# An attention, MLP and routed-expert kernel: new transfer times in the planner of the routed part, later take-up of weights, low parts on one engine, a regrouped end

## The chip, the cores and the metric

One core of a Trainium2 chip runs the whole program. The metric is the device time of one execution, in microseconds; a profiled execution is also given, with the span from its first to its last instruction. The engines are named as the profile names them: PE (TensorE matmul), PEld (its weight loads), DVE (VectorE), ACT (ScalarE), POOL (GpSimd) and SP (SyncE, which issues most transfers).

## What is computed

Windowed attention with memory tokens, then a two-layer MLP with leaky ReLU, then eight experts of which each token takes exactly one. The experts are filled by a greedy pass over all (token, expert) scores in falling order, each expert up to `cap = 384` tokens, so which expert a token gets can't be told from its own scores alone.

```python
def _moe2_ref(x, w_gate, w1, w2):              # x: 3072 x 512, E = 8, F = 1024
    logits = x @ w_gate
    order = np.argsort(-logits.flatten())
    for idx in order:
        tok, e = int(idx) // E, int(idx) % E
        if assigned[tok] >= 0 or counts[e] >= cap:
            continue
        assigned[tok] = e
        counts[e] += 1
    for e in range(E):
        mask = assigned == e
        out[mask] = np.maximum(x[mask] @ w1[e], 0.0) @ w2[e]
```

## The kernel before, in words

All matmuls of the MLP and the experts are made of three passes on rounded operands: a high part and a low part of each operand, high by high, high by low and low by high. A high part is an ACT copy, a low part is the difference, usually on DVE.

Nothing of the order of work is written out by hand. Every step is handed to a planner (`Plan`) with the engine it runs on, an assumed duration in microseconds, its dependencies and a priority (`key`, smaller first). `Plan.run` plays the assumed durations through and emits the instructions of each engine in the order in which the play starts them. On the chip every engine then works strictly through its own list and waits by semaphores. An assumed duration therefore changes no work, only the order of the lists. Transfers are played as ops of a single engine "D", one after the other, first ready first, and land 1.1 us plus the D time after their issue. `late=` adds to the time at which an op is held to be ready; `after=` lets an op be placed only once the named ops have been placed.

The change touches the routed part, `phase2`. For each expert in the order in which they fill up (p = 0 to 7):

- `search(p)` finds which expert fills next and at which score, by six rounds of threshold search. A round is a chain of small steps between DVE and PE: `differ` (tile d), `compare` (cm), `count` on PE (L311, pc), `less` (lc), `threshold` (fl), `base` on PE (L332, pb). It has the highest priority. Search p+1 starts when search p is done; the last expert needs none.
- `number(p)` reads the expert's number into a register of SP, `tail(p)` turns the tokens' places into indices (sl, sp, A, rh, then `tokens` on PE at L458), gathers 384 rows (`xg`, three transfers from POOL, L473), transposes them on PE (L478) and writes high and low parts (ACT `xth` L481, DVE `xtl` L485). These parts together are `XT[p]`, and every gemm1 of the expert waits for them.
- `load(p, f)` fetches slice f of eight (w1 and w2 slice side by side, 512 KB) into a ring of four `west` buffers, or for p = 0 as two halves into a ring of three. ACT makes the high part (L590) and DVE or POOL the low part (L591), two halves each. The weights of an expert alternate between two places, so they carry the names `wh`, `wl` (odd p) and `winh`, `winl` (even p).
- `gemm1(p, f)` is 12 matmuls (L608); ACT and DVE turn the result into `egh` (L614) and `egl` (L615). `gemm2(p, f)`, two slices later, is 9 matmuls (L631), three for each of the three tiles i of 128 tokens, which gather over all f in three accumulators.
- With the last slice each tile is copied out by ACT (`x`, L641) and stored row by row by POOL (L646), a 1x1 memset (L645) ahead of each store.

Priorities: loads have `200 + 8p + f - 6`, gemm1 `200 + 8p + f`, gemm2 two more; searches, tails and numbers are far below zero. While the MLP ends and the routed part's first rows come in, 40 matmuls that compute nothing (L659) keep PE going.

Of the kernel before, what the change touches and what calls it, by code (L numbers as in the profile page):

```python
# [15 lines left out]
AF = mybir.ActivationFunctionType  # L16
# [198 lines left out]
def phase2(tc, P, C, ident, L, x2d, we, out, ps_h, ps_o, ps_y, pools, lready, xready, open_pools, open_experts, room, roomy, before):  # L215
# [7 lines left out]
    NTILE, E = L.shape[1], L.shape[2]  # L223
    DM = out.shape[1]
    KD = DM // 128
    NF = we.shape[2]
    TT = NTILE // E
    TB = TT * 128
    FMAX = 3.4e38
    LASTV = 5  # L230
    LATE, SLACK = 0.3, 0.7
    SW = 0.12
    V, G, S = nc.vector, nc.gpsimd, nc.scalar
# [186 lines left out]
    def ranks(p):  # L420
        r = R[p]
        r["ps"] = pools["ps_t"].tile([128, 1], FT, name="pt")
        nc.tensor.matmul(r["ps"], C[0]["tri"], r["fx"][:, NTILE:], start=True, stop=True)

    def slots(p):

        r = R[p]
        b = rt([128, NTILE], FT, "sb")
        a = rt([128, NTILE], I16, "sl")
        V.tensor_scalar(b, r["fx"][:, :NTILE], r["ps"], 32.0, op0=OP.add, op1=OP.add)  # L430
        V.tensor_tensor(a, b, r["F"], op=OP.mult)
        s = r["sl"] = rt([128, 2, NTILE], I16, "sp")
        V.tensor_scalar(s[:, 0], a, 31, None, op0=OP.bitwise_and)
        V.tensor_scalar(s[:, 1], a, 5, None, op0=OP.logical_shift_right)

    def places(p):
        c, r = C[0], R[p]
        W = NTILE // PACK
        r["A"] = rt([128, PACK, 32, W], F16, "A")
        V.tensor_tensor(r["A"], c["i32"][:, :, :W][:, None].to_broadcast([128, PACK, 32, W]),  # L440
                        r["sl"][:, 0].rearrange("p (a b) -> p a b", a=PACK)[:, :, None, :]
                        .to_broadcast([128, PACK, 32, W]), op=OP.is_equal)

    def parts(p):
        c, r = C[0], R[p]
        oc = rt([128, 12, NTILE], F16, "oc")
        V.tensor_tensor(oc, c["i32"][:, 1:13], r["sl"][:, None, 1].to_broadcast([128, 12, NTILE]), op=OP.is_equal)
        r["rh"] = rt([128, 12, NTILE], F16, "rh")
        V.tensor_tensor(r["rh"], oc, c["token"][:, None, :].to_broadcast([128, 12, NTILE]), op=OP.mult)

    def tokens(p):

        r = R[p]
        W = NTILE // PACK
        r["px"] = pools["ps_t"].tile([128, PACK, TT, 4], FT, name="pt")
        A, rh = r["A"], r["rh"].rearrange("p n (a b) -> p a n b", a=PACK)
        for j in range(W):
            nc.tensor.matmul(r["px"], A[:, :, :, j].rearrange("p a m -> p (a m)"), rh[:, :, :, j],  # L458
                             start=(j == 0), stop=(j == W - 1))

    def indices(p):
        r = R[p]
        r["idx"] = rt([128, TT], I32, "idx", 4)
        s = rt([32, 2, TT, 4], FT, "ix")
        blk = lambda a: r["px"][32 * a:32 * a + 32, a]
        V.tensor_scalar(s[:, 0], blk(0), float(HALF), None, op0=OP.add)
        V.tensor_tensor(s[:, 1], blk(1), s[:, 0], op=OP.add)
        V.tensor_tensor(s[:, 0], blk(2), s[:, 1], op=OP.add)
        for n in range(4):
            V.tensor_tensor(r["idx"][32 * n:32 * n + 32], blk(PACK - 1)[:, :, n], s[:, 0, :, n], op=OP.add)  # L470
# [5 lines left out]
    def transpose(b, x):  # L476
        for d in range(KD):
            nc.tensor.transpose(b.t[:, d * 128:(d + 1) * 128], x.t[:, d * 128:(d + 1) * 128], ident)  # L478
# [23 lines left out]
    X, XT = {}, {}  # L502

    def small(us, fn, deps, use=(), late=0.0):

        return P.op(("T", us + SW), fn, deps, use, early=SW, late=late)
# [27 lines left out]
    def tail(p):  # L534
        P.key = -1000 + 10 * p + (1 if p else -1)
        late = SLACK if p else 0.0
        o = small(0.04, lambda: ranks(p), [filled[p], tchain], late=late)
        o = P.op(("V", 0.67), lambda: slots(p), [o])
        ts = [P.op(("V", 0.47), lambda: places(p), [o]), P.op(("V", 0.6), lambda: parts(p), [o])]
        o = small(0.53, lambda: tokens(p), ts, late=late)  # L540
        o = P.op(("V", 1.25), lambda: indices(p), [o])
        gathered[p] = o
        xg, gs = [], []
        for i in range(TT):
            x = r_xg[i].take()
            g = P.op(("G", 1.25), lambda i=i, x=x: gather(p, i, x), [o, xready, open_experts], [x])
            d = P.op(("D", 0.73), None, (), [x])
            P.dep(d, [g], lat=4.6 if p else 2.9)
            xg.append(x)
            gs.append(d)  # L550
        X[p] = [r.take() for r in r_xt]
        XT[p] = []
        for i in range(TT):
            b = ps_h.take() if p == 0 and i else Buf(lambda: pools["ps_t"].tile([128, DM], FT, name="pt"), None, None)
            o = small(0.44, lambda i=i, b=b: transpose(b, xg[i]), [gs[i], [] if p == 0 else o], [xg[i], b], late=late)
            a = P.op(("S", 0.5), lambda i=i, b=b: xhi(i, b, X[p]), [o], [X[p][0], b])
            o = P.op(("V", 0.6), lambda i=i, b=b: xlo(i, b, X[p]), [a], [*X[p], b])
            XT[p] += [a, o]
        tchain[:] = [o]


    W, REG = {}, {}
# [7 lines left out]
        REG[p] = P.op(("Q", 2.0), fn, [filled[p]])  # L570

    def load(p, f):
        P.key = 200 + NF * p + f - 6
        w = [r.take() for r in r_w[f]]
        n = 2 if p == 0 else 1
        d = []
        for b in [(ps_y if p == 0 else r_west).take() for _ in range(n)]:
            c = slice(1024 // n * len(d), 1024 // n * (len(d) + 1))

            def fn(b=b, c=c):  # L580
                src = we[bass.ds(R[p]["reg"], 1)].rearrange("a p f d -> (a p) f d")
                nc.sync.dma_start(b.t, src[:, f, c])

            d.append((b, P.dma(1.46 / n, fn, [REG[p]], [b], [open_experts if p else roomy[f]])))
        o = []
        for h in range(2):
            sl = slice(512 * h, 512 * h + 512)
            b, l = d[h % n]
            raw = lambda b=b, h=h: b.t if n == 2 else b.t[:, 512 * h:512 * h + 512]
            a = P.op(("S", 0.53), lambda sl=sl, raw=raw: S.activation(w[0].t[:, sl], raw(), AF.Copy), [l], [b, w[0]])  # L590
            o.append([a, P.op({"G": 1.22, "V": 0.6} if p == 0 else {"V": 0.6, "G": 1.22} if p > LASTV else {"V": 0.6}, lambda e=V, sl=sl, raw=raw: e.tensor_tensor(  # L591
                w[1].t[:, sl], raw(), w[0].t[:, sl].bitcast(FT), op=OP.subtract), [a], [b, *w])])
        W[p, f] = w, o

# [26 lines left out]
    def gemm2(p, f):  # L621
        s = NF * p + f
        P.key = 200 + s + 2
        w, o = W[p, f]
        gh, gl, done = GL.pop(s)
        if f == 0:
            ACC[p] = [r.take() for r in ps_o]

        def mm(i, n):
            l, a = ((gh, 0), (gh, 1), (gl, 0))[n]  # L630
            nc.tensor.matmul(ACC[p][i].t, l.t[:, 128 * i:128 * i + 128], w[a].t[:, 512:1024],  # L631
                             start=(f == 0 and n == 0), stop=(f == NF - 1 and n == 2))

        for i in range(TT):
            for n in range(3):
                q = PREV[i] = P.op(("T", 0.231), lambda i=i, n=n: mm(i, n), [done[:1 + n // 2], o[1], PREV.get(i)],
                                   [ACC[p][i], gh, gl, *w])
            if f < NF - 1:
                continue
            y = ps_y.take()  # L640
            o2 = P.op(("S", 0.53), lambda i=i, y=y: S.activation(y.t, ACC[p][i].t, AF.Copy), [q], [ACC[p][i], y])  # L641

            def fn(i=i, y=y):
                if stores:
                    G.memset(rt([1, 1], FT, "spacer"), 0.0)  # L645
                st = G.indirect_dma_start(  # L646
                    out=out, out_offset=bass.IndirectOffsetOnAxis(ap=R[p]["idx"][:, i:i + 1], axis=0),
                    in_=y.t, in_offset=None)
                for other in stores:
                    tc.declare_no_dep(st.ins, other.ins, reason="a token has one expert: rows of other tokens")  # L650
                stores.append(st)

            o2 = P.op(("G", 1.04), fn, [o2], [y])
            P.dep(P.op(("D", 0.73), None, (), [y]), [o2], lat=1.2)


    b, o = ps_h.take(), before
    for _ in range(40):
        prev, o = o, P.op(("T", 0.22), lambda b=b: nc.tensor.matmul(b.t[:, :128], ident, ident, start=True, stop=True),  # L659
                          (), [b], key=1e6)  # L660
# [603 lines left out]
```

## Time and profile before

| | us |
|---|---|
| three runs | 1025.14, 1026.04 (median), 1030.17 |
| the profiled execution's own time | 1028.83 |
| its span | 1027.0 |
| PE busy, of the span | 990.3 (96%) |
| DVE busy | 779.9 (76%) |
| ACT busy | 440.9 (43%) |
| POOL busy | 145.6 (14%) |
| chain that ended last: share of PE, DVE, transfers | 74%, 11%, 6% |

The routed part is the last 337 us of the span: its first gemm1 stands at 689.8, its last matmul at 1018.8. Busy shares here say little, since matmuls overlap in the records. What says more is the timeline of PE with the idle time ahead of each instruction and its releaser, and then, for each such gap, the timeline of the engine that released it, followed backwards.

### The profile page before, as it was taken

How to read it: one execution, taken by the hardware profiler on the slowest of the kernel's cores; microseconds unless marked ns; L12 is line 12 of the kernel's file. 1: busy time of each engine (PE TensorE's matmuls, PEld its weight loads, DVE VectorE, ACT ScalarE, POOL GpSimd, SP SyncE). 2: the span in 40 equal slices, each digit the busy share in tenths (PEclk: the TensorE clock that was granted, in tenths of full speed). 3: DMA queues.
4: the chain of work that ended last, by engine and by line, in shares of the span. 5: the costliest groups of instructions: out<-in, count | busy, mean ns of one | idle time of the engine just before them, and what ended most of it. 6: DMA issues, size and time to landing. Idle time of an engine off the chain costs nothing.

```text
span 1027.0 us, 17361 instructions
## 1 busy us (share of the span) xinstructions
PE 990.3 (96%) x6052; PEld 861.3 (84%) x6052; DVE 779.9 (76%) x2631; ACT 440.9 (43%) x1183; POOL 145.6 (14%) x155
## 2 busy tenths in 40 slices
PE   8799999999999999999999999989999999899996
PEld 7687888888888888888889988778778787788895
DVE  7999798788788698798788664688786887867610
ACT  6677634434434434543544333043342523326411
POOL 1677520000000000000000000011111211112311
PEclk9799999999999999999999999999999999989998
DMA  7666510110111120120120000155152432508400
GB/s 240 217 217 215 188 51 30 60 57 29 60 57 29 50 67 29 43 74 29 31 68 1 1 1 32 52 175 174 52 195 76 170 135 102 195 32 281 139 31 31
DMA packets 36326, 95.48 MB, mean 93 GB/s; under 512 B 4368, under 2 KB 8464, under 8 KB 36112
## 3 DMA queue, kind: packets, MB, share of 16 engines
q1 hardware_dynamic: 32400, 81.80, 23.7%
q0 software_dynamic: 3840, 12.59, 3.7%
q8 instruction: 47, 0.77, 0.3%
q14 instruction: 39, 0.32, 0.1%
HBM read 81.79 MB, written 12.58 MB: 92 GB/s over the span
## 4 chain that ended last, share of the span: by engine, by line
PE 74%; DVE 11%; DMA 6%; issue 5%; ACT 3%; POOL 1%; DVEq 0%; POOLq 0%; ACTq 0%; SPq 0%
PE po L1028 24%; PE ph L935 23%; PE ph L608 9%; PE po L631 8%; DMA west<-in_we_dram 4%; PE pa L814 3%; PE pa L887 2%; PE pa L864 2%; DVE wl L591 2%; DVE wa L914 2%; DVE wp L912 2%; PE pc L311 1%; DVE winl L591 1%; DMA x<-in_we_dram 1%; DVE wp L911 1%
## 5 line engine op out<-in xcount | busy, mean ns | idle before, releaser
L1058 DVE CUSTOM_DVE_ANT_0 junk<-x,wgb 128x512 bf16<-128x512 f32 x296 | 206.4, 697 | 4.0 <-ACT x L1042 0.3
L943 ACT ACTIVATE gs<-ph 128x384 f32<-128x384 f32 x128 | 62.6, 489 | 211.1 <-PE ph L935 202.3
L1028 PE MATMUL po<-woutl,gh 128*128 128x512 f32 x336 | 134.2, 400 | 1.4 <-POOL woutl L919 1.4
L1028 PE MATMUL po<-wouth,gh 128*128 128x512 f32 x336 | 135.3, 403 | 0.0
L1028 PE MATMUL po<-wouth,gl 128*128 128x512 f32 x336 | 131.3, 397 | 0.1
L944 DVE TENSOR_TENSOR gs<-ph,gs 128x384 f32<-128x384 f32 x128 | 70.9, 555 | 77.2 <-ACT gs L943 76.4
L935 PE MATMUL ph<-x1h,winh 128*128 128x384 f32 x512 | 112.2, 341 | 1.5 <-DVE x1h L855 1.1
L935 PE MATMUL ph<-x1h,winl 128*128 128x384 f32 x512 | 111.8, 340 | 0.0
L935 PE MATMUL ph<-x1l,winh 128*128 128x384 f32 x512 | 110.6, 337 | 0.0
L826 ACT ACTIVATE X<-X,st 96x128 f32<-96x128 f32 x248 | 96.3, 390 | 31.5 <-DVE st L823 31.5
L935 PEld LDWEIGHTS ph<-x1h,winh 128*128 128x128 f32 x512 | 92.4, 189 | 11.6 <-DVE x1h L855 1.4
L935 PEld LDWEIGHTS ph<-x1h,winl 128*128 128x128 f32 x512 | 92.8, 190 | 1.2 <-POOL winl L919 0.2
L935 PEld LDWEIGHTS ph<-x1l,winh 128*128 128x128 f32 x512 | 91.6, 190 | 0.4
L614 ACT ACTIVATE egh<-ph 128x384 fp32r<-128x384 f32 x64 | 31.3, 489 | 141.0 <-PE ph L608 127.2
L1028 PEld LDWEIGHTS po<-wouth,gl 128*128 128x128 f32 x336 | 63.0, 188 | 13.6 <-POOL gl L946 0.7
L1028 PEld LDWEIGHTS po<-woutl,gh 128*128 128x128 f32 x336 | 63.2, 188 | 13.1 <-POOL woutl L919 2.8
L1028 PEld LDWEIGHTS po<-wouth,gh 128*128 128x128 f32 x336 | 63.1, 188 | 13.2 <-POOL wouth L917 0.2
L945 ACT ACTIVATE gh<-gs 128x384 fp32r<-128x384 f32 x112 | 58.4, 521 | 34.1 <-DVE gs L944 33.6
L615 DVE SCALAR_TENSOR_TENSOR egl<-ph,egh 128x384 fp32r<-128x384 f32 x64 | 35.5, 554 | 48.4 <-ACT egh L614 48.2
L818 DVE CUSTOM_DVE_ANT_0 X<-pa,masks 96x128 f32<-96x128 f32 x232 | 57.2, 280 | 5.9 <-PE pa L814 5.9
L1143 POOL IOTA ij<- 128x128 int32 x1 | 0.2, 234 | 400.9 <-DVE L L1058 400.9
L946 DVE TENSOR_TENSOR gl<-gs,gh 128x384 fp32r<-128x384 f32 x87 | 47.9, 552 | 11.3 <-ACT gh L945 11.2
(247 smaller groups left out, 1975.2 us busy)
## 6 DMA issues: line engine op xcount, KB each, us to landing
west<-in_we_dram SPq DMA_DIRECT2D x56, 512.0 KB, 5.1
wst<-in_w_dram SPq DMA_DIRECT2D x32, 512.0 KB, 4.2
kt<-in_k_dram SPq DMA_DIRECT2D x31, 256.0 KB, 3.5
vt<-in_v_dram SPq DMA_DIRECT2D x30, 256.0 KB, 2.6
qt<-in_q_dram SPq DMA_DIRECT2D x31, 192.0 KB, 3.1
x2d<-x SPq DMA_DIRECT2D x21, 256.0 KB, 2.3
x<-in_we_dram SPq DMA_DIRECT2D x16, 256.0 KB, 3.2
wgb<-in_w_gate_t_dram SPq DMA_DIRECT2D x1, 2048.0 KB, 7.1
```

Source lines behind the costliest of these rows:

```text
L608: nc.tensor.matmul(ph.t[:, :TB], w[a].t[:, k * 128:(k + 1) * 128], xs[x].t[:, k, :], start=(n == 0), stop=(n == 3 * KD - 1))
L615: b = P.op(("V", 0.47), lambda: V.scalar_tensor_tensor(gl.t, ph.t[:, :TB], 0.0, gh.t.bitcast(FT), op0=OP.max, op1=OP.subtract), [a], [ph, ...
L631: nc.tensor.matmul(ACC[p][i].t, l.t[:, 128 * i:128 * i + 128], w[a].t[:, 512:1024], start=(f == 0 and n == 0), stop=(f == NF - 1 and n == 2))
L818: V.tensor_tensor_reduce(out=X.t[:, h, :], in0=ps[h % 2].t[:QB, h // 2 * 128:h // 2 * 128 + 128], in1=masks[:, var, :], scale=1.0, scalar= ...
L826: S.activation(X.t[:, h, :], X.t[:, h, :], AF.Exp, bias=st.t[:, 1, h:h + 1], scale=scale, accum_out=st.t[:, 2, h:h + 1])
L935: nc.tensor.matmul(ph.t[:, :TB], win[wt][:, f, kk * 128:(kk + 1) * 128], xt.t[:, kk, :], start=(n == 0 and kk == 0), stop=(n == 2 and kk = ...
L943: o = P.op(("S", 0.37), lambda: S.activation(t.t, ph.t[:, :TB], AF.Copy, scale=0.01), [o], [ph, t], key=k)
L944: o = P.op(("V", 0.47), lambda: V.tensor_tensor(t.t, ph.t[:, :TB], t.t, op=OP.max), [o], [ph, t], key=k)
L945: x = P.op(("S", 0.42), lambda: S.activation(gh(), t.t, AF.Copy), [o, gd], [t, *gb], key=k)
L946: y = P.op({"V": 0.47} if j > 1 else {"V": 0.47, "G": 0.96} if j else {"G": 0.96}, lambda e=V if j > 1 else G: e.tensor_tensor(gl(), t.t, ...
L1028: nc.tensor.matmul(acc.t, lt()[:, sl], wout[wt][:, f, :], start=(f == 0 and n == 0), stop=(n == 2 and (f == NF - 1 or s == S6 - 1)), skip_ ...
L1058: V.tensor_tensor_reduce(out=pools["wgb"].tile([128, DM], BF, name="junk"), in0=x, in1=WGB[0][:, e, :], scale=1.0, scalar=0.0, op0=OP.mult ...
```

## The change

It edits only `phase2`:

- planned D times: a load 2.2 instead of 1.46 (halved for the halves of expert 0), a gather 1.05 instead of 0.73, a store 1.05 instead of 0.73 with 1.6 instead of 1.2 of latency;
- the high part of a load is held ready 2.0 later than its landing, for every expert but the first;
- low parts run on DVE alone: before, the planner chose between DVE and POOL for experts 0, 6 and 7;
- for expert 0 the loads of slices 4 to 7 get a key of 4 more, and their high parts are placed only after `XT[0]`;
- for the last expert the keys of gemm2 of slices 6 and 7 go by tile first and slice second.

```diff
-    LASTV = 5
+    FIRST = 4
+    HOLD = 2.0
@@ tail
-            d = P.op(("D", 0.73), None, (), [x])
+            d = P.op(("D", 1.05), None, (), [x])
             P.dep(d, [g], lat=4.6 if p else 2.9)
@@ load
-        P.key = 200 + NF * p + f - 6
+        P.key = 200 + NF * p + f - (6 if p or f < FIRST else 2)
...
-            d.append((b, P.dma(1.46 / n, fn, [REG[p]], [b], [open_experts if p else roomy[f]])))
+            d.append((b, P.dma(2.2 / n, fn, [REG[p]], [b], [open_experts if p else roomy[f]])))
...
-            a = P.op(("S", 0.53), lambda sl=sl, raw=raw: S.activation(w[0].t[:, sl], raw(), AF.Copy), [l], [b, w[0]])
-            o.append([a, P.op({"G": 1.22, "V": 0.6} if p == 0 else {"V": 0.6, "G": 1.22} if p > LASTV else {"V": 0.6}, lambda e=V, sl=sl, raw=raw: e.tensor_tensor(
+            a = P.op(("S", 0.53), lambda sl=sl, raw=raw: S.activation(w[0].t[:, sl], raw(), AF.Copy), [l], [b, w[0]],
+                     XT[0] if p == 0 and f >= FIRST else (), late=HOLD if p else 0.0)
+            o.append([a, P.op(("V", 0.61), lambda sl=sl, raw=raw: V.tensor_tensor(
                 w[1].t[:, sl], raw(), w[0].t[:, sl].bitcast(FT), op=OP.subtract), [a], [b, *w])])
@@ gemm2
         for i in range(TT):
+            if p == E - 1 and f >= NF - 2:
+                P.key = 200 + NF * p + NF + 1 + i + (f - NF) / 4
@@ gemm2, store
-            P.dep(P.op(("D", 0.73), None, (), [y]), [o2], lat=1.2)
+            P.dep(P.op(("D", 1.05), None, (), [y]), [o2], lat=1.6)
```

## Rows read from the trace of the kernel before

**Rows 1.** Timeline of PE: start, length, instruction, count, idle before and releaser.

```profile
721.39 0.45 PE L311 MATMUL pc<-oh,cm 128*128 128x32 bf16 x6 [0.72 <-DVE cm L299]
...
763.71 0.16 PE L332 MATMUL pb<-fl,ones 32*128 32x1 bf16 x1 [1.65 <-DVE fl L328]
...
899.14 0.46 PE L311 MATMUL pc<-oh,cm 128*128 128x32 bf16 x6 [3.13 <-DVE cm L299]
...
948.04 0.97 PE L608 MATMUL ph<-xth,winh 128*128 128x384 f32 x4 [1.36 <-ACT xth L481]
954.46 0.69 PE L458 MATMUL pt<-rh,A 128*128 128x48 f16 x6 [1.83 <-DVE rh L449]
```

**Rows 2.** Timeline of ACT and DVE ahead of the gap that ends at 899.14.

```profile
897.02 0.63 ACT L590 ACTIVATE wh<-west 128x512 fp32r<-128x512 f32 x1 [2.31 <-DMA west<-in_we_dram]
897.55 0.47 ACT L614 ACTIVATE egh<-ph 128x384 fp32r<-128x384 f32 x1
898.06 0.56 DVE L615 SCALAR_TENSOR_TENSOR egl<-ph,egh 128x384 fp32r<-128x384 f32 x1 [2.26 <-ACT egh L614]
```

**Rows 3.** Waits of ACT, 700 to 950: sum in us, times, longest.

```profile
ACT wh L590 <- DMA west<-in_we_dram: 17.6, 12, 2.3
ACT winh L590 <- DMA west<-in_we_dram: 10.7, 8, 2.3
```

**Rows 4.** Windows: stretch, length, PE, PEld, DVE, ACT, POOL busy, PEclk, DMA share, GB/s.

```profile
763.00:768.00 5.00, 4.29 (x23) 3.81 (x23) 4.90 (x14) 3.02 (x7) 0.00 (x0) 0.72 0.05 17
899.00:904.00 5.00, 4.86 (x19) 3.99 (x20) 3.91 (x13) 1.67 (x4) 0.00 (x0) 0.50 0.00 0
926.00:948.00 22.00, 20.67 (x109) 17.80 (x107) 15.73 (x35) 13.77 (x27) 5.45 (x7) 1.00 0.87 305
```

**Rows 5.** Tile west, 690 to 990, and the timeline of SP's issues for two experts.

```profile
DMA to landing us min/median/max: 3.5/5.1/7.8
...
926.26 31.33 SPq L582 DMA_DIRECT2D west<-in_we_dram  x16
```

**Rows 6.** Timeline of PE and DVE where expert 3 begins.

```profile
816.01 0.60 PE L478 MATMUL pt<-ident,xg 128*128 128x128 f32 x4
817.32 0.69 DVE L485 TENSOR_TENSOR xtl<-pt,xth 128x512 fp32r<-128x512 f32 x1
818.16 0.86 PE L608 MATMUL ph<-xth,wh 128*128 128x384 f32 x4
```

**Rows 7.** Timeline where POOL makes low parts, and line 431 over the whole span.

```profile
950.14 2.54 POOL L591 TENSOR_TENSOR wl<-west,wh 128x512 fp32r<-128x512 f32 x2 [0.81 <-ACT wh L590]
950.21 1.27 DVE L431 TENSOR_TENSOR sl<-sb,F 128x24 int16<-128x24 f32 x1
951.51 1.20 DVE L433 TENSOR_SCALAR sp<-sl 128x24 int16<-128x24 int16 x1
...
L431 DVE TENSOR_TENSOR sl<-sb,F x8: 183/184/1266, 663.1 to 950.2; 128x24 int16<-128x24 f32 x8
```

**Rows 8.** Timeline of the end, from gemm2 of the last expert's slice 6.

```profile
1014.91 0.39 PE L631 MATMUL po<-wh,egh 128*128 128x512 f32 x1
...
1017.83 1.96 ACT L641 ACTIVATE x<-po 128x512 f32<-128x512 f32 x3 [4.31 <-PE po L631]
...
1018.71 0.97 POOL L646 DMA_INDIRECT out_dram<-x,idx  x1 [25.56 <-ACT x L641]
...
1021.25 0.97 POOL L646 DMA_INDIRECT out_dram<-x,idx  x1 [0.21 <-issue]
```

**Rows 9.** Timeline of ACT and PE where expert 0 begins.

```profile
688.61 0.63 ACT L590 ACTIVATE winh<-x 128x512 fp32r<-128x512 f32 x1 [0.82 <-DMA x<-in_we_dram]
689.15 0.58 ACT L481 ACTIVATE xth<-ph 128x512 fp32r<-128x512 f32 x1
...
689.78 0.97 PE L608 MATMUL ph<-xth,winh 128*128 128x384 f32 x4 [0.42 <-ACT xth L481]
```

**Rows 10.** Groups by line, 690 to 990: busy us, mean ns.

```profile
L591 DVE TENSOR_TENSOR wl<-west,wh 128x512 fp32r<-128x512 f32 x61 | 40.4, 678 | 1.8 <-ACT wh L590 1.6
```

## The prediction

> **What bounds the kernel now.** I read the timeline of PE through the routed part first, because there the idle time and its releaser stand beside each instruction. From the first gemm1 to the last matmul PE has thirteen gaps between 0.2 and 3.13 us, 12.2 us in all; the first, the largest and the last are shown [rows 1]. Eleven of them, 9.0 us together, lie before 948 and are released by DVE: PE, which works through its list in order, stands at a small matmul of the search (or once a transpose) whose input DVE has not made. So PE bounds the part, and the search sets how often it stops.
>
> Next I followed the largest gap backwards through DVE and ACT [rows 2]. DVE was idle for 2.26 us in front of `egl`, with the search's `cm` queued behind it; `egl` waited for `egh` on ACT; and `egh` stood behind a high part of a weight that itself had been idle for 2.31 us until its transfer landed. The same chain, one copy shorter, ends in the 1.65 us gap at 763.71. The wait that ends last is therefore not the search's own work but a landing that the planner had put too early. The waits of ACT say how common that is: between 700 and 950 it stood 20 times for a `west` transfer, 28.3 us in all [rows 3]. Why, the transfers tell: a load takes 5.1 us from issue to landing in the median and up to 7.8 [rows 5], while the plan counts 1.1 + 1.46 = 2.6.
>
> Last, the clock. After the two long gaps the granted clock falls to the lower of its two levels, 1.2 GHz, and comes back within the stretch: it averages 0.72 over 763 to 768 and 0.50 over 899 to 904 [rows 4]. PE had work there, so the two stretches lose about 5 x 0.28 = 1.4 and 5 x 0.50 = 2.5 us.
>
> **The change part by part.** All terms are against the profiled execution, 1028.83 us (span 1027.0), which is 0.27% above the median of the runs, 1026.04; the result is scaled by 0.9973.
>
> *New times and the later take-up.* No instruction, transfer or semaphore wait is added; only the lists change. With the change the plan counts 1.1 + 2.2 + 2.0 = 5.3 us from issue to take-up, just over the median landing of 5.1 and 2.5 short of the longest [rows 5]. So most of ACT's 20 waits go, and with them the hold on `egh`, `egl` and the search's step behind them. At stake are the eleven gaps, 9.0, and the 3.9 of the clock: 12.9 us. Not all can go: the longest landings stay late, and some of the eleven are small gaps in which DVE is merely busy with low parts, which stay as many (0.68 us each [rows 10], 16 an expert). I take seven tenths, 9.0 us; the ends are 12.9 and nothing.
>
> The cost: a load holds the planned "D" for 2.2 us, and a gather that becomes ready behind it is planned later. Behind the gathers come the transposes, ACT and DVE copies of `XT`, and every gemm1 of the next expert. Where expert 3 begins there is no cover left: the last transpose starts at 816.01, its low part ends at 818.01, and the first gemm1 follows at 818.16, the time between filled to the end with gemm2 of the expert before [rows 6]. A gather behind one load is planned 0.74 + 0.32 = 1.1 us later, behind three 2.5 us; four experts (3 to 6) begin so tightly. That is 0 to 10 us. But from the second transpose on the chain of `XT` itself, not the gather, sets the pace, and a search freed from ACT starts its gathers sooner. I take 2.4 us as loss, 0.6 an expert.
>
> The rate of the transfers speaks against the 2.2: 16 loads were issued within 31.3 us [rows 5], 1.96 each, while the core moved 305 GB/s with gathers and stores among them [rows 4]; 0.524 MB at 305 GB/s is 1.7 us. So 2.2 each in a row plans the last of eight loads up to 4 us too late; what that would do is the third rival. The Trainium skill, "DMA: Bandwidth & Descriptors", Specifications, puts the limit of HBM for one core at about 358 GB/s, by which a load would take 1.46 us (an estimate), the old planned time, and the last of eight would be planned 5.9 us too late; by that rule the loss of 2.4 would be some 3.6. The trace comes close to that limit, with 305 GB/s over 22 us, and doesn't pass it.
>
> Holding `west` longer delays SP's next issues: four buffers, each taken for about 5.1 of landing, up to 2 of hold and some 2 of copying, give a load every 2.3 us, so eight take 18 us, against at most 16 x 1.96 / 2 = 16 now. Slice 7 is needed only seven slices of matmuls after slice 0, so I cost these 2 us at nothing; without that cover they would be paid for each expert.
>
> *Low parts on DVE alone.* Only three low parts ran on POOL at all, two of them at 950; none for expert 0. While POOL ran these two, `sl` took 1.27 us and `sp` 1.20 on DVE, against 0.184 for `sl` in the median [rows 7]. Those are 2.1 us of a chain that goes on through A and rh to the matmul at 954.46, for which PE idled 1.83 us [rows 1]. Back on DVE the three cost 3 x 0.68 = 2.0 us, of which later take-up puts most behind that chain. Gain 0 to 1.83; I take 1.5.
>
> *The last slices tile by tile.* Now gemm2 of slices 6 and 7 runs from 1014.91 in 18 matmuls to about 1019.0, 0.229 each, slice by slice. Tile 0 is ready after 12, is copied at 1017.83 and stored at 1018.71; POOL's stores then follow at 1.27 us each, so the last starts at 1021.25 though its copy ended at 1019.79 [rows 8]. By tiles, tile 0 is ready after 6 matmuls: 6 x 0.229 = 1.37 us sooner. Its store starts at 1017.34, the next at 1018.7, the last when its own copy allows, 1019.79 + 0.24 = 1020.03: 1.2 us sooner, and POOL has kept its queue empty. `egl` of slice 7 is made while gemm2 of slice 5 runs, before it is needed either way. Gain 1.2; the ends are 0.6 (if the scheduling puts a wait between) and 1.3.
>
> *Expert 0.* The transposed third tile waits on ACT behind a weight copy that waits for a transfer: idle 0.82, then 0.63 of copy, then `xth` at 689.15 and gemm1 at 689.78 [rows 9]. With slices 4 to 7 behind `XT[0]`, that 1.45 us goes, and up to 2.5 if the DVE's low parts around it also leave. But the start of expert 0 helps only as far as the first search ends sooner too, and eight low parts (5.4 us) move into its second half. On SP five half loads are issued later, ahead of expert 1's; slice 4 is used only after four gemm1 and two gemm2, which covers them. Between -2 (loss) and 2.5; I take 0.7, nearer to the row's 1.45.
>
> Sum: -9.0 + 2.4 - 1.5 - 1.2 - 0.7 = -10.0, so 1018.8, scaled 1016.0 us. The stall that remains largest should be the start of expert 6 (1.36 us now [rows 1]).
>
> **The rivals.** *The search catches up wholly.* All of the 12.9 go, the gap at 948.04 with them, the 1.83, the 1.2 and the 2.5, and the gathers cost nothing: -19.8, that is 1006.3. For it speaks that all eleven gaps have one source; against it, that DVE still makes 16 low parts an expert among the search's steps.
>
> *Only the local edits bite.* The gaps are then DVE's own load, and freeing ACT moves them only elsewhere: -1.5 - 1.2 - 0.7 and at most 0.6 of the rest, -4.0, that is 1022. For it: DVE's low parts sit between the search's steps whatever ACT does.
>
> *The plan now waits for gathers that have landed.* The planned time is too long, as the rows on the rate suggest, the gathers queue behind up to three loads, and at experts 3 to 6 PE runs dry for 2.5 us each: +10.2, with 1.4 of clock each time as after the gap at 763: +5.6. Against that half of the 12.9 and the local 3.4 remain: -9.9. That is +5.9, or 1032. It decides from about 2.5 us lost at each of the four starts, the clock included. Against it: the plan's search moves on in the meantime, and today's gathers land late as well.
>
> **How the numbers follow.** Forecast 0.50 at 1016, its own range 1010 to 1021; the catch-up 0.17 at 1006; local only 0.20 at 1022; gathers 0.13 at 1032. About what a measurement of this kernel can tell from no change is 0.5%, 1020.9 to 1031.2. Faster takes 0.47 of the forecast, 0.17 and 0.05 of the local case: 0.69. Same: 0.03, 0.15 and 0.03: 0.21. Slower: 0.10 of the last. The range from 1007 to 1028 leaves out about half of the catch-up case and most of the last.
>
> **What would show it.** Right: ACT's waits for `west` fall from 28.3 us to under 8; no gap of PE over 1.7 us between 700 and 950 and no half clock after 700 before the end; `sl` at 0.18 for every expert; stores at the end each following their own copy; gemm1 of expert 0 before 689. Wrong: ACT's waits gone but PE's gaps still released by DVE (local only); gaps in front of gemm1 with `xth` or a transpose as releaser at experts 3 to 6 (gathers); or the first search ending later than now.

## The result, and the profile after

| | before | after |
|---|---|---|
| median of four runs, us | 1027.57 | 1009.39 (1008.78 to 1010.50) |
| ratio of the times, with its 95% interval | | 0.984 (0.981 to 0.987) |
| profiled execution, own time / span | 1028.83 / 1027.0 | 1008.78 / 1007.0 |

The change gains 18.2 us between the medians, 20.0 between the two spans. The forecast was 1016.0, a gain of 10.0: the direction held and the time lies inside the range, but the forecast gain was little more than half of what the chip gave.

The first lines of the page of the changed kernel (each engine's busy time, share of the span and instructions):

```profile
span 1007.0 us, 17359 instructions
PE 984.0 (98%) x6052; PEld 859.0 (85%) x6052; DVE 778.4 (77%) x2634; ACT 439.6 (44%) x1183; POOL 141.1 (14%) x152
```

PE's busy time fell by 6 us and the span by 20. Where the 20 lie is read from two windows that begin with the first gemm1 of the routed part and end with its last matmul (stretch, length, busy PE, PEld, DVE, ACT, POOL, PEclk, DMA share, GB/s). The kernel before:

```profile
689.78:1019.16 329.38, 316.83 (x1773) 269.78 (x1773) 224.65 (x765) 118.26 (x222) 51.79 (x67) 0.98 0.36 124
```

and the changed kernel:

```profile
689.48:1000.29 310.81, 309.47 (x1759) 266.42 (x1759) 223.47 (x760) 119.36 (x228) 48.57 (x66) 1.00 0.41 135
```

Ahead of this stretch 0.3 us are gained, in it 18.6, behind it 1.1 (from 7.84 to 6.71 us). Of the 18.6, 11.2 are idle time of PE (12.55 before, 1.34 after) and 7.4 are busy time. The matmuls in the two windows are not quite the same: 1773 before, 1759 after, since 14 small ones of a search come ahead of the first gemm1 in the changed kernel.

The waits of ACT for weights from 690 to 950 after the change (engine, line, what for: sum in us, times, longest), against [rows 3]; the first line is the half loads of expert 0, the second is `west`:

```profile
ACT winh L591 <- DMA x<-in_we_dram: 3.6, 3, 1.4
ACT wh L591 <- DMA west<-in_we_dram: 0.7, 2, 0.5
```

and the landing of `west`, 690 to 990, against the first of [rows 5]:

```profile
DMA to landing us min/median/max: 3.6/4.7/6.9
```

The transfers land nearly as late as before (5.1 in the median, 7.8 at most [rows 5]), but ACT stands for them twice and not 20 times. The one idle stretch of PE over 0.1 us that is left after the first gemm1 has this row in PE's timeline; it answers to the fourth of [rows 1]:

```profile
931.15 0.96 PE L610 MATMUL ph<-xth,winh 128*128 128x384 f32 x4 [1.15 <-ACT xth L482]
```

The end of the changed kernel, ACT's copies and POOL's stores, against [rows 8]:

```profile
997.60 0.60 ACT L645 ACTIVATE x<-po 128x512 f32<-128x512 f32 x1 [2.95 <-PE po L633]
998.48 0.97 POOL L650 DMA_INDIRECT out_dram<-x,idx  x1 [24.21 <-ACT x L645]
...
999.84 0.97 POOL L650 DMA_INDIRECT out_dram<-x,idx  x1 [0.30 <-ACT x L645]
1000.32 0.60 ACT L645 ACTIVATE x<-po 128x512 f32<-128x512 f32 x1 [0.76 <-PE po L633]
...
1001.20 0.97 POOL L650 DMA_INDIRECT out_dram<-x,idx  x1 [0.30 <-ACT x L645]
```

Every store now follows its own copy. The last one starts 0.9 us after the last matmul's end; before it was 2.1.

### The profile page after: what moved, and what is told of

Read it like the earlier page. It is cut to its first block, busy times and chain, and to the rows that moved or that the text cites. A ratio compares the mean times of both kernels' runs of the same rounds, so it can differ in the third digit from the quotient of the medians.

```text
span 1007.0 us, 17359 instructions
## 1 busy us (share of the span) xinstructions
PE 984.0 (98%) x6052; PEld 859.0 (85%) x6052; DVE 778.4 (77%) x2634; ACT 439.6 (44%) x1183; POOL 141.1 (14%) x152
## 4 chain that ended last, share of the span: by engine, by line
PE 84%; DVE 7%; issue 4%; ACT 2%; POOL 1%; DMA 0%; POOLq 0%; DVEq 0%; ACTq 0%
PE po L1032 25%; PE ph L939 24%; PE ph L610 12%; PE po L633 11%; PE pa L818 3%; PE pa L891 2%; PE pa L868 2%; PE pc L312 2%; DVE wa L918 2%; DVE wp L916 1%; DVE wp L915 1%; PE pt L479 1%; ACT X L830 1%; PE ph L663 1%; POOL out_dram L650 0%
## 5 line engine op out<-in xcount | busy, mean ns | idle before, releaser
L950 DVE TENSOR_TENSOR gl<-gs,gh 128x384 fp32r<-128x384 f32 x87 | 47.9, 552 | 11.3 <-ACT gh L949 11.2
```

Source lines behind the costliest of these rows:

```text
L950: y = P.op({"V": 0.47} if j > 1 else {"V": 0.47, "G": 0.96} if j else {"G": 0.96}, lambda e=V if j > 1 else G: e.tensor_tensor(gl(), t.t, ...
```

## The experiments

The first set takes the change apart, the second asks which number of the planning carries the gain, the third disturbs the landings themselves. "Stretch" below is the time from the first gemm1 to the last matmul, "idle" PE's idle time in it, both from windows as above; "west" is ACT's sum of waits for `west` from 690 to 950. Ratios are against the kernel before, run beside them on the same chip: 1027.57 us for the changed kernel's first row, then 1025.81, 1025.93 and 1024.89 for each four rows in turn.

| kernel | median us | ratio (95%) | stretch | idle | west |
|---|---|---|---|---|---|
| before | 1027.57 | 1 | 329.4 | 12.6 | 28.3 |
| after | 1009.39 | 0.984 (0.981 to 0.987) | 310.8 | 1.3 | 0.7 |
| times and take-up alone | 1007.27 | 0.982 (0.980 to 0.985) | 309.6 | 0.0 | 1.3 |
| expert 0's edit alone | 1030.22 | 1.004 (1.003 to 1.006) | 330.4 | 14.7 | 29.6 |
| low parts and last slices alone | 1021.59 | 0.995 (0.993 to 0.997) | 329.7 | 13.0 | 28.4 |
| after, without expert 0's edit | 1005.41 | 0.979 (0.977 to 0.982) | 309.6 | 0.2 | 1.4 |
| after, once more | 1007.85 | 0.982 (0.979 to 0.985) | 312.0 | 1.3 | 0.5 |
| without expert 0's edit, once more | 1005.17 | 0.979 (0.977 to 0.982) | 309.3 | 0.0 | 1.4 |
| take-up alone | 1012.22 | 0.987 (0.984 to 0.989) | 314.5 | 2.8 | 6.8 |
| times alone | 1007.10 | 0.981 (0.978 to 0.983) | 310.0 | 0.3 | 5.1 |
| the loads' number alone | 1006.57 | 0.983 (0.979 to 0.987) | 310.0 | 0.2 | 10.7 |
| loads at 0.8 | 1035.07 | 1.010 (1.007 to 1.013) | 330.0 | 13.9 | 37.3 |
| half loads | 1016.90 | 0.993 (0.990 to 0.996) | 319.6 | 7.2 | 12.8 |
| after, no expert 0's edit, no take-up | 1006.50 | 0.982 (0.978 to 0.985) | 309.7 | 0.3 | 4.0 |

### Times and take-up alone

The kernel before with the planned times and the later take-up, nothing else:

```diff
+    HOLD = 2.0
...
-            d = P.op(("D", 0.73), None, (), [x])
+            d = P.op(("D", 1.05), None, (), [x])
...
-            d.append((b, P.dma(1.46 / n, ...
+            d.append((b, P.dma(2.2 / n, ...
...
-            a = P.op(("S", 0.53), ..., [l], [b, w[0]])
+            a = P.op(("S", 0.53), ..., [l], [b, w[0]], late=HOLD if p else 0.0)
...
-            P.dep(P.op(("D", 0.73), None, (), [y]), [o2], lat=1.2)
+            P.dep(P.op(("D", 1.05), None, (), [y]), [o2], lat=1.6)
```

> The kernel before with the new planned times (2.2, 1.05, 1.05) and the later take-up (2.0) alone. Theory A (landings planned too early stop ACT, and ACT stops the search): ACT's waits for west fall from 28.3 us (700 to 950) to under 3, the eleven gaps of PE before 948 and both half-clock stretches go, and the time falls by 11 to 14 us, ratio 0.986 to 0.990. Rival B (the first search, which ends 5.8 us sooner in the changed kernel, is what carries the gain on to the end): most of the gaps stay, the time falls by 3 to 6 us, ratio 0.994 to 0.997.

It reaches 0.982, as much as the whole change and more than the 11 to 14 us of Theory A. Its window from the first gemm1 to the last matmul:

```profile
687.82:997.42 309.60, 309.60 (x1763) 265.80 (x1761) 223.52 (x760) 117.56 (x223) 46.88 (x66) 1.00 0.40 133
```

PE has no idle time left in 309.6 us. The gain is that of the planning; the three local edits together add nothing to it that the time shows, since one of them loses what another gains (below). POOL still made two low parts here, one at the start of expert 0 and one at 924.8; the second was over before `sl`, so nothing in the chain of expert 6's tail was slowed.

### Expert 0's edit alone

```diff
+    FIRST = 4
...
-        P.key = 200 + NF * p + f - 6
+        P.key = 200 + NF * p + f - (6 if p or f < FIRST else 2)
...
-            a = P.op(("S", 0.53), ..., [l], [b, w[0]])
+            a = P.op(("S", 0.53), ..., [l], [b, w[0]], XT[0] if p == 0 and f >= FIRST else ())
```

> The kernel before with expert 0's slices 4 to 7 placed behind XT[0] (and their later key) alone. Theory A: the first search ends at about 696 instead of 701.7, but later searches still stop at ACT's waits for west, which stay at 20 to 30 us; the time falls by no more than the lead, 3 to 6 us, ratio 0.994 to 0.997. Rival B: the lead of the search empties the later gaps too, under 4 us of gaps are left, and the time falls by 10 us or more, ratio under 0.990.

It is a loss, 0.4% with an interval clear of 1, where both theories had a gain. The first gemm1 stands at 690.56, no sooner than before, and the stretch keeps all its stalls. The "first search" of these texts is `search(1)`, the first to end after the first gemm1, and the "second" is `search(2)`; a search is counted as ended here when the expert's number (tile `ei`) is written. `search(1)` ends 0.9 us later than before. ACT waits for landings as long as ever, and one stall of PE became the largest of any kernel here (first the waits of ACT, 690 to 950, then a row of PE's timeline):

```profile
ACT wh L591 <- DMA west<-in_we_dram: 18.0, 9, 4.6
ACT winh L591 <- DMA west<-in_we_dram: 11.6, 9, 2.5
```

```profile
809.96 0.16 PE L333 MATMUL pb<-fl,ones 32*128 32x1 bf16 x1 [3.96 <-DVE fl L329]
```

### Low parts on DVE and the last slices, alone

```diff
-            o.append([a, P.op({"G": 1.22, "V": 0.6} if p == 0 else ... {"V": 0.6}, ...
+            o.append([a, P.op(("V", 0.61), ...
...
+            if p == E - 1 and f >= NF - 2:
+                P.key = 200 + NF * p + NF + 1 + i + (f - NF) / 4
```

> The kernel before with all low parts on DVE and the last expert's slices 6 and 7 tile by tile, alone. Theory A: the gap of 1.83 us ahead of the matmul of tokens of the last expert goes, sl takes 0.18 us there, and the last store starts about 1.2 us after where it would by its own copy: the time falls by 2 to 3 us, ratio 0.997 to 0.998; the eleven earlier gaps stay. Rival: the three low parts on DVE cost what they save and the end alone is won, 1.2 us.

The ratio is 0.995, with single times from 1017.4 to 1026.2. The trace says where the part lies that is sure. The stretch is as long as before (329.7 against 329.4). Behind it, 6.7 us are left where 7.8 were: 1.2 us, from the stores. The medians lie 4.2 us apart; the other 3 are not in this trace, which is that of the slowest of the ten executions, and stay open. `sl` takes 0.184 us for every expert, and the stall in front of `tokens` is gone; but PE's idle time in the stretch is 13.0, not less, for the start of expert 6 took over what was freed, and the two largest stalls (2.48 and 3.58) are longer than before (two rows of PE's timeline, at expert 6):

```profile
946.09 0.66 PE L478 MATMUL pt<-ident,xg 128*128 128x128 f32 x4 [1.06 <-DVE xtl L485]
948.38 0.98 PE L608 MATMUL ph<-xth,winh 128*128 128x384 f32 x4 [1.63 <-ACT xth L481]
```

### The change without expert 0's edit

```diff
-    FIRST = 4
+    FIRST = 8
```

> The changed kernel with expert 0's loads as before (key and place). Theory A: terms add up, so the time is 4 to 6 us above the changed kernel's, ratio to the kernel before 0.988 to 0.990, gaps of PE between 700 and 930 still under 2 us in all. Rival B: without the lead of the first search the gaps come back, ratio 0.993 or more.

With FIRST at 8 no load of expert 0 is moved. The time falls below that of the whole change, which neither theory had. As the two had not stood side by side, both ran again on one chip.

> The changed kernel itself, beside the one without expert 0's edit, on one chip. Theory A2 (new: expert 0's edit costs time, since eight low parts are pushed into the time of the next search): it comes out 2 to 5 us above the kernel without that edit. Rival C (the edit is neutral, and the difference between the two earlier ratios is that of two jobs): within 1.5 us of it.

> The changed kernel with expert 0's loads as before, again, as partner of the run above. Theory A2: ratio to the kernel before 0.978 to 0.981, and 2 to 5 us below the changed kernel. Rival C: within 1.5 us of it.

There: 1007.85 with the edit, 1005.17 without, so the edit costs 2.7 us; the two intervals overlap a little (0.979 to 0.985 and 0.977 to 0.982). The traces show where. The low parts of expert 0 between the ends of `search(1)` and `search(2)` (696 to 741; duration min/median/max in ns, first and last start), in the changed kernel:

```profile
L593 DVE TENSOR_TENSOR winl<-x,winh x5: 670/680/682, 701.1 to 714.1; 128x512 fp32r<-128x512 f32 x5
```

Without the edit there is none there: its last one starts at 694.0. So five low parts, 5 x 0.68 = 3.4 us of DVE, move into `search(2)`. `search(1)` gets shorter by the edit (34.1 us from the end of the search before it, against 36.3) and `search(2)` longer (44.2 against 38.8). The end of the search that finds expert 6 then comes 16.8 us after the first gemm1 of expert 5, against 12.3 without the edit, and PE runs dry at the start of expert 6: the 1.15 us shown above. The second trace of the changed kernel shows another cost. Ahead of the first gemm1 PE waits 1.00 us for the search in both traces of it (shown under expert 0 below), and in neither trace without the edit. Behind that wait the clock was granted in full in the first trace, but in the second it was at the lower level, 1.2 GHz, for most of 689 to 693, about 1.7 us lost. How often that happens the two traces don't tell. Without the edit no stall is left there (window of the kernel without the edit, second time):

```profile
687.14:996.44 309.30, 309.30 (x1763) 265.42 (x1761) 223.12 (x762) 117.62 (x223) 45.87 (x66) 1.00 0.41 133
```

### Which number of the planning: take-up alone, times alone, loads alone

The take-up alone:

```diff
+    HOLD = 2.0
...
-            a = P.op(("S", 0.53), ..., [l], [b, w[0]])
+            a = P.op(("S", 0.53), ..., [l], [b, w[0]], late=HOLD if p else 0.0)
```

> The kernel before with the later take-up of 2.0 us alone: the plan counts 2.6 + 2.0 = 4.6 us from a load's issue to its take-up where the measured median is 5.1. Theory A (what counts is that the plan takes a weight up no sooner than it lands): most of the waits go, ACT's waits for west 3 to 10 us instead of 28, and 8 to 14 us of the 18 are won, ratio 0.986 to 0.992. Rival D (what counts is the planned rate of the transfers, since later landings of a burst run ahead of the plan by several us): waits of 15 us or more stay and under 6 us are won.

The times alone:

```diff
-            d = P.op(("D", 0.73), None, (), [x])
+            d = P.op(("D", 1.05), None, (), [x])
...
-            d.append((b, P.dma(1.46 / n, ...
+            d.append((b, P.dma(2.2 / n, ...
...
-            P.dep(P.op(("D", 0.73), None, (), [y]), [o2], lat=1.2)
+            P.dep(P.op(("D", 1.05), None, (), [y]), [o2], lat=1.6)
```

> The kernel before with the new planned transfer times alone: 1.1 + 2.2 = 3.3 us for a first load, but each further load of a burst 0.74 later than before. Theory A: between the two, as the first loads of each expert still come too early: ACT's waits 8 to 18 us, 4 to 10 us won, ratio 0.990 to 0.996. Rival D: waits under 6 us, 12 us or more won, ratio 0.988 or less.

The loads' number alone:

```diff
-            d.append((b, P.dma(1.46 / n, ...
+            d.append((b, P.dma(2.2 / n, ...
```

> The kernel before with one number changed: a weight load is planned at 2.2 us on the DMA engines instead of 1.46; the gathers' and the stores' planned times stay. Theory A (the loads' number is what matters): about 1007, ACT's waits for west under 5 us, at most one gap, as with all the times changed (1007.1). Rival (the gathers' and the stores' numbers bring a good part, since the gathers stand in the same planned queue): over 1011, with gaps around the gathers (3 to 6 us) left.

The take-up alone brings 0.987, as its Theory A had it; the times alone bring 0.981, as the rival had it and not Theory A; the loads' number alone brings 0.983. So the gathers' and the stores' numbers carry nothing that shows, and the single constant of the load carries all. The take-up alone stays some 5 us behind. Where the two differ most is `search(1)`: HOLD excepts expert 0, and that search takes 40.3 us with it and 36.2 with the times alone (39.8 before). Whether that exception or the slower pace at which the larger constant plans the loads of a burst makes the difference was not tried apart. Besides, with the take-up alone four small stalls are left, 2.5 us, the largest at the start of expert 6 (row of PE's timeline):

```profile
932.95 0.97 PE L610 MATMUL ph<-xth,winh 128*128 128x384 f32 x4 [1.09 <-ACT xth L482]
```

A point against too simple a reading: with the loads' number alone ACT still waits 10.7 us for `west`, more than with the take-up alone (6.8), and PE idles only 0.2 us (window):

```profile
686.30:996.27 309.97, 309.80 (x1763) 265.76 (x1761) 222.85 (x761) 117.12 (x223) 48.39 (x65) 1.00 0.39 132
```

So not each wait of ACT costs PE something. Two of these seven waits, 3.8 us, come at 938 and 942, after the last search's end at 898.8, where there is no search left to hold. That the other five stand where they hold no step that PE needs is argued from PE's idle time, not followed one by one.

### The opposite dose: a load planned at 0.8

```diff
-            d.append((b, P.dma(1.46 / n, ...
+            d.append((b, P.dma(0.8 / n, ...
```

> The opposite dose: the kernel before with a weight load planned at 0.8 us instead of 1.46. Theory A (planned earlier than it lands, the work stalls on the landing): ACT's waits for west above the 28 us of before, gaps ahead of gemm1 above 15 us, the time 3 to 10 us above the kernel before, 1029 to 1036. Rival (the stalls don't come from the load's planned time): within 2 us of the kernel before.

ACT's waits rise to 37.3 us and the time by 1.0%, as the first theory had it; but the stretch is only 0.6 us longer than before and the stalls hardly more (13.9 against 12.6; above 15 was expected). The spans of the two profiled executions differ by 4.3 us, and most of that lies ahead of the first gemm1, which comes at 693.46, 3.7 us later than before (4.2 later, counted from the end of `search(0)`). The medians are 10 us apart, so the rest of the loss is in neither of these two traces. The same mechanism shows there, in the half loads of expert 0 (timeline of ACT and PE):

```profile
681.67 0.63 ACT L590 ACTIVATE winh<-x 128x512 fp32r<-128x512 f32 x1 [2.97 <-DMA x<-in_we_dram]
683.69 1.30 ACT L590 ACTIVATE winh<-x 128x512 fp32r<-128x512 f32 x2 [1.39 <-DMA x<-in_we_dram]
684.90 0.58 ACT L481 ACTIVATE xth<-pt 128x512 fp32r<-128x512 f32 x1
...
690.68 0.60 PE L478 MATMUL ph<-ident,xg 128*128 128x128 f32 x4
...
693.46 0.99 PE L608 MATMUL ph<-xth,winh 128*128 128x384 f32 x2
```

`xth` of the first tile, whose transpose was done by 682.5, stands behind three copies, with 2.97 and 1.39 us of waiting for their transfers, until 684.90 (682.22 in the kernel before), and what comes behind it moves back. So planning too early costs; below 1.46, the stretch itself had little more to lose.

### Half loads

The loads of experts 1 to 7 fetch half the columns; planner and lists are those of the kernel before. The kernel leaves out the second layer's weights of these experts, and the first layer's are copied twice in their place.

```diff
-                nc.sync.dma_start(b.t, src[:, f, c])
+                if n == 1:
+                    nc.sync.dma_start(b.t[:, :512], src[:, f, 0:512])
+                else:
+                    nc.sync.dma_start(b.t, src[:, f, c])
...
-            raw = lambda b=b, h=h: b.t if n == 2 else b.t[:, 512 * h:512 * h + 512]
+            raw = lambda b=b, h=h: b.t if n == 2 else b.t[:, :512]
```

> The kernel before with its own planned times, but every weight load of experts 1 to 7 fetches only the first 512 of its 1024 columns (256 KB instead of 512 KB) and both copies read these; part of the computation is left out, the second layer's weights of those experts, so the time is that of a kernel with half the routed weight traffic. The order of the work on every engine is meant to stay. Theory A (the stalls of the kernel before are landings that come later than planned): ACT's waits for west between 700 and 950 us fall from 28 us to under 10, most of the gaps ahead of gemm1 (14 to 16 us in the kernel before) go, and the time falls by 8 to 14 us, to 1012 to 1018. Rival B (the stalls come from the order in which the work is put on the engines, and the landings only happen to end last): gaps of over 6 us stay, and the time falls by under 5 us.

Nothing is planned differently here; only the landing comes sooner (tile `west`, 690 to 990; then ACT's waits, 690 to 935):

```profile
DMA to landing us min/median/max: 2.6/3.4/4.6
```

```profile
ACT wh L593 <- DMA west<-in_we_dram: 7.0, 9, 1.8
ACT winh L593 <- DMA west<-in_we_dram: 4.2, 5, 1.8
```

The time falls by 0.7% (7 to 8 us), the stretch by 9.8: at the lower edge of what the first theory gave, and not the under 5 of its rival. ACT's waits fall by more than half but not under 10 (12.8 up to 950), which fits a landing of 3.4 us against the 2.6 planned. Of 7.2 us idle, more than the 6 that the rival had set as its mark, 4.15 are two rows that no landing made alone:

```profile
935.01 0.96 PE L611 MATMUL ph<-xth,winh 128*128 128x384 f32 x4 [1.36 <-ACT xth L481]
942.39 0.68 PE L458 MATMUL pt<-rh,A 128*128 128x48 f16 x6 [2.79 <-DVE rh L449]
```

These are the start of expert 6 and the `tokens` step behind POOL's low parts, as in the last two of [rows 1]. The stalls ahead of them fall from 9.0 to 2.9 us in all. So the larger part of the stalls were late landings and not the order as such. What the order adds beyond them this kernel doesn't tell, since a landing that was earlier still wasn't tried.

### Without the take-up

The change without expert 0's edit, and HOLD at 0:

```diff
-    FIRST = 4
-    HOLD = 2.0
+    FIRST = 8
+    HOLD = 0.0
```

> The changed kernel without expert 0's edit and with HOLD at 0: planned times, low parts on DVE alone and the last slices tile by tile remain. Theory A (the times alone carry the gain of the planning, the later take-up adds nothing to them): about 1005, the same as with HOLD 2.0 (1005.2 to 1005.4), ACT's waits for west 2 to 6 us, at most one gap. Rival (the take-up still covers late landings that the times leave): 1008 or more, with two or more gaps.

1006.50, against 1005.17 and 1005.41 with the take-up, which did not run beside it. By the ratios, 0.982 against 0.979, the take-up would add some 2 us once the times are right, by the medians 1.1 to 1.3; the intervals overlap, so neither is sure. The best kernel of the study is the change without expert 0's edit, 0.979 (0.977 to 0.982) both times, ahead of the change as it was made, though the intervals overlap a little.

## Why the prediction was right, and where its steps were not

*What bounds the kernel* was read rightly: landings put too early, passed on by ACT to `egh`, to DVE and to the search. Five kernels show it from different sides: one constant for the load takes the stalls away, a smaller one makes more waits, shorter transfers under old lists take most of the stalls away, and the two with edits that leave the planned landings alone keep the stalls (14.7 and 13.0 us). One reading was off a little: of the eleven gaps two stood at a transpose (0.35 and 0.20 us), not one.

*New times and take-up*: the term that was mis-sized. The prediction put 12.9 us at stake, took seven tenths (9.0) and set 2.4 against it, net 6.6. Alone these edits gave 0.982, 18 us, and 19.8 in the stretch. That the forecast's range still held the time is in part luck: this term was some 12 us too small, and the terms for expert 0 and for the low parts were together some 5 too good. Four things were missing in it.

- All eleven gaps went, not seven tenths. The reason given for a rest, small gaps in which DVE is merely busy with low parts, didn't hold: DVE makes as many low parts as before (16 an expert) and PE idles 0.0 us. Most of those small gaps were therefore late landings at second hand. With the half loads, whose lists are the old ones, nine gaps of 0.27 to 0.37 us are left, 2.9 in all; whether these are the order or landings that are still late is open.
- The gap in front of `tokens`, 1.83, went with them too: POOL could still make low parts, but under the new lists its late one was over before `sl`.
- The clock was worth more than 3.9. Both windows of [rows 4] ended inside the slow stretch; the next ones of the kernel before show it going on, to 768.6 and 905.2 (stretch, length, busy times, PEclk):

```profile
768.00:770.00 2.00, 2.00 (x9) 1.56 (x9) 1.84 (x9) 0.42 (x1) 0.00 (x0) 0.84 0.00 0
904.00:906.00 2.00, 2.00 (x8) 1.31 (x7) 0.84 (x3) 0.00 (x0) 0.00 (x0) 0.71 0.00 0
```

  That is another 2 x 0.16 + 2 x 0.29 = 0.9, or 4.8 us in all. The half loads bear it out: with the same lists, 1775 matmuls in the stretch and no slow clock, PE is busy there for 312.4 us, 4.4 less than the kernel before. In the profiled execution after the change no slow stretch lies between the first gemm1 and the last matmul; in the second trace of that kernel one does, from 689 on, as told above.
- From 316.8 to 309.5 us of busy time are 7.4, and the clock explains up to 4.8. Of the other 2.6 about 1 us are the 14 small matmuls that lie in the stretch only before the change (a `count` of 12 takes 0.88 us). What is left, an estimated 1.5 us, is not explained; it may be idle time that the records count as busy where the stream of matmuls is broken.

*The gathers' loss* of 2.4 was nothing, and with it the third rival fell. At expert 3 the border is as tight as in [rows 6], without a gap (timeline of PE and DVE after the change):

```profile
806.83 0.60 PE L479 MATMUL pt<-ident,xg 128*128 128x128 f32 x4
...
809.34 0.68 DVE L486 TENSOR_TENSOR xtl<-pt,xth 128x512 fp32r<-128x512 f32 x1
...
810.41 0.78 PE L610 MATMUL ph<-xth,wh 128*128 128x384 f32 x3
```

From the end of its search to the first gemm1 of expert 3 pass 27.4 us here (27.6 before), and over the six starts of experts 1 to 6 together 162 (165 before). The loss had been worked out for gathers alone, as if the search before them stood still. It ended sooner: `search(3)` ends 14.6 us after the first gemm1 of expert 2, and before it was 18.2. In the kernel without expert 0's edit 28.6 us pass at experts 2 to 5, a microsecond more, and PE still has no gap there. By the Trainium skill, "DMA: Bandwidth & Descriptors", Specifications, a load of 512 KB would take an estimated 1.46 us at the 358 GB/s that it gives as the limit, the old planned number, and the rule drawn from it would have made the 2.2 a greater loss, 3.6. The runs decide against it: the one constant brought 18 us. A rate says how often loads can land, not when each one does: 4.7 to 5.2 us after its issue in the median, in the four kernels in which it was read (before, after, the loads' number alone, loads at 0.8). Even 2.2 counts only 3.3 us for the first load of a burst, so the runs don't show that the landing itself is the best number to plan with.

*Low parts on DVE alone*: forecast 1.5, measured nothing that the trace can show. `sl` fell to 0.184 as forecast, but alone it only passed the stall on, and with the new times the stretch is 309.6 with or without it (309.3 in a second trace with it).

*The last slices by tile*: forecast 1.2, measured 1.1 to 1.2, from the mechanism as it was told: the time from the last matmul's end to the end of the span fell from 7.84 to 6.71, and in the kernel with only the local edits to 6.66.

*Expert 0*: forecast a gain of 0.7, between a loss of 2 and a gain of 2.5. It is a loss, 2.7 within the whole change and some 4 alone. The step that failed is "that 1.45 us goes": gemm1 of expert 0 came at 689.48, not before 689. ACT does take up the third tile at once, but the tile itself is transposed 0.4 us later than before (687.32 there), so `xth` comes 0.8 sooner. And PE, in the order of its list, then stands for 1.00 us at a step of the search until DVE has made `g`, with gemm1 of expert 0 queued behind it (timeline after the change, against [rows 9]):

```profile
687.74 0.60 PE L479 MATMUL ph<-ident,xg 128*128 128x128 f32 x4
688.37 0.60 ACT L482 ACTIVATE xth<-ph 128x512 fp32r<-128x512 f32 x1 [4.63 <-PE ph L479]
...
689.45 0.34 PE L348 MATMUL pc<-g,ones 128*128 128x384 bf16 x1 [1.00 <-DVE g L343]
689.48 0.99 PE L610 MATMUL ph<-xth,winh 128*128 128x384 f32 x4
```

The caution in the same paragraph, low parts that move into the second half of expert 0, named the right cost, but tied it to the first search, `search(1)`; it was `search(2)` that paid.

*The rivals.* The catch-up had the right mechanism and, at 1006, nearly the right time; without expert 0's edit it is met (1005.2), in part by luck, as its sum holds 2.5 us for expert 0. The forecast gave it too little because it kept a share of the stalls for DVE's own load. "Only the local edits bite" fell with the edits that were tried alone.

*What was to be seen*: ACT's waits under 8 (0.7), no gap over 1.7 (1.15), `sl` at 0.18 for every expert, stores each after their copy, and the start of expert 6 as the largest stall left all came; gemm1 of expert 0 before 689 did not in this trace. The row for `sl` over the changed kernel's whole span:

```profile
L432 DVE TENSOR_TENSOR sl<-sb,F x8: 183/183/184, 663.1 to 933.2; 128x24 int16<-128x24 f32 x8
```

## What to carry to other kernels

Where lists are ordered by assumed durations, check the assumed time of a transfer against the time from issue to landing that the trace shows under load, and don't plan with bytes over a rate: here one constant, raised by half, was worth 18 us, and the finer edits together nothing more, a gain of 1.2 and a loss of 2.7 among them. Which part of the larger number does it, the later landing or the slower pace, the runs don't separate in full. When many small stalls on one engine trace back to one cause, count them in, also those whose releaser merely looks busy, and add the clock that comes with them. An edit that frees the start of a chain has to be followed to where its work goes: five low parts out of the first search were paid for in the second.

## What the runs showed of the hardware

The granted clock of PE didn't follow the length of the last gap alone. In the kernel before, the lower level (0.50, 1.2 GHz) came after gaps of 1.65 and 3.13 us [rows 1, 4] and not after those of 1.36 and 1.83; in the half loads a gap of 2.79 us left it at full speed, both in the 7 us that hold most of the gap and in the 8 us behind (windows):

```profile
935.00:942.00 7.00, 4.59 (x25) 4.24 (x26) 6.90 (x12) 6.01 (x12) 4.91 (x6) 1.00 0.53 164
942.00:950.00 8.00, 7.61 (x43) 7.07 (x43) 7.82 (x20) 3.75 (x8) 3.57 (x4) 1.00 0.44 126
```

Two executions of one kernel show it too. In those of the changed kernel, PE's wait of 1.00 us ahead of the first gemm1 is followed by the full clock in one and by the lower level in the other (windows, the first trace and then the second):

```profile
689.40:693.00 3.60, 3.55 (x21) 3.40 (x22) 3.44 (x15) 1.62 (x4) 0.00 (x0) 1.00 0.28 72
689.00:692.00 3.00, 3.00 (x11) 3.00 (x11) 2.84 (x15) 0.92 (x2) 0.00 (x0) 0.51 0.28 74
```

A load of 512 KB took 5.1 us from issue to landing in the median, one of 256 KB 3.4 in the same place, so halving the bytes took off a third. The Trainium skill, "DMA: Bandwidth & Descriptors", Anatomy of one DMA — SWDGE (gpsimd) path, has a fixed 2.0 us and 436 GB/s for another way of issuing, by which an estimate would be 3.2 and 2.6; with several loads under way on SP's queue both take longer than that.

`sl` and `sp` on DVE took 1.27 and 1.20 us while POOL made low parts [rows 7], and 0.18 and 0.17 without in the median (one `sp` of the changed kernel took 0.41, while POOL issued a store). The Trainium skill, "SBUF — State Buffer", Who interferes with whom, says that a DVE instruction with two inputs in SBUF contends with a GpSimd instruction that reads SBUF, and that this contention is an exclusive lock; `sl` has two such inputs, and the trace agrees. `sp` has one and was held as long; that sentence alone doesn't tell why, and no run here took the two apart.
